# Attention ahead of two feed-forward layers on one core: scores in four two-bank units, transposes and products with v regrouped

## The chip, the cores and the metric

The kernel runs on one core of a Trainium2 chip. The metric is the device time of one execution in microseconds (us), the median of several runs. Engines are named as the profile names them: PE is the matrix engine (PEld its loading of weights), DVE the vector engine, ACT the scalar engine, POOL the GpSimd engine, SP the sync engine, which issues nearly all transfers here.

## What is computed

Attention with a decay per key (batch 4, 8 heads, 576 positions, 64 per head), then two feed-forward layers on the 2304 tokens, all in float32:

```python
scores = scale * q @ k.T                       # scale 1/8
cum = cumsum(log(clip(f, 1e-4, 1)))
scores = where(causal, -1e9, scores + cum[:, None] - cum[None, :])
attn = exp(scores - max(scores)); attn = attn / (sum(attn) + 1e-9)
x = attn @ v                                   # heads side by side: 2304 x 512
h = x @ w_in;  x = (h - tanh(h)) @ w_out       # 512 -> 2048 -> 512
h = x @ w_in2; out = (h * sigmoid(h)) @ w_out2
```

## The kernel before

Two heads make a pair, one on partitions 0 to 63 and one on 64 to 127; there are 16 pairs. The 576 queries of a head are cut into four tiles of 128 (i = 0 to 3; tile i sees 128(i+1) keys) and a last 64, and the last 64 of both heads share one tile, called i = 4, of 576 keys. So a pair has nine tiles, and the attention has 144. Each tile takes one step of a loop (`for n in range(N + LAG + 9)`, L643), and every engine works in the order in which this loop writes its instructions; nothing is reordered later.

A tile goes through these functions. `scores` (L429) and `scores_tail` (L440) multiply on PE in float32r: q and k are split in a high and a low part (`kqs`, made by `split` on POOL and DVE), and four products (high-high, high-low, low-high, decay rows) are added in PSUM. The two heads' products use 64 rows of the array each and run side by side. `least` (L452) adds the mask on DVE, copies the scores out of PSUM and finds the row's extreme. `expo` (L473) takes the exponential on ACT. `guard` and `normalise` (L480, L484) make the reciprocals of the row sums on DVE for three tiles at once, and POOL multiplies the tiles by them. `transposes` (L491) turns the tile in blocks of 128 x 128 on PE, nine steps after its scores (LAG = 9). `evac` (L514) copies them from PSUM to `ptf`, on ACT where i is 3 or 4, on DVE otherwise. `values` (L518) multiplies with v on PE with 64 columns of the array for each head, in four parts spread over nine steps, and `collect` (L530) copies the sums to x on ACT.

PSUM has eight banks: four of one tile each for scores (`ps_s`), two for transposes (`ps_t`), `misc` (half of tile 4's scores, and the first 64 queries' products with v) and `out_t`. A bank is written again when the instruction that reads it has ended. PE thus changes between three uses of its array: 64 rows for a head (scores), the whole array (transposes, tile 4, fillers, the layers) and 64 columns for a head (products with v).

Transfers are issued by SP in order: `load_kq` (608 KB a pair, `kqraw`), `load_v` (320 KB, `vraw`), `place_last` (the last 64 queries into `lq`, out of `kqs`), `place_dec` and `place_dec_last` (decay rows into `de` and `lq`). Pair 0 has its decay rows from `rows` in SBUF; these are also written to memory (`dec`), and all later pairs read them there. During the first nine steps `busy` puts idle matmuls of 512 columns between the steps of PE.

Weights come as float64 bits (512 KB for each half of a chunk, `raw`) and are decoded on ACT, DVE and POOL (`wstages`: L154 to L181) into high and low parts. Two chunks are decoded during the attention, three more from step 145 on, while the first hidden products (`hidden`, L256) already run between the last transposes; after the loop `front` and `project` (L315) follow without a break.

Of the kernel before, what the change touches and what calls it, by code (L numbers as in the profile page):

```python
# [23 lines left out]
LAG = 9  # L24
# [16 lines left out]
def forgetting_attention_two_ffn(  # L41
# [25 lines left out]
    def setup_masks(const):  # L67
# [9 lines left out]
        mask4 = const.tile([P, S // 2], F32, name="mask4")  # L77
        nc.gpsimd.memset(mask4, 0.0)
        for j in range(2):
            m = mask4[64 * j:64 * j + 64, S // 2 - 64:]  # L80
# [247 lines left out]
    def attention():  # L328
        with ExitStack() as actx:
# [8 lines left out]
            sp = pool(actx, "sp", LAG + 1)  # L338
# [7 lines left out]
            ps_s = pool(early, "ps_s", 4, space=PSUM)  # L346
# [11 lines left out]
            s4, out_0 = misc[:, 0:S // 2], misc[:, 448:512]  # L358
# [52 lines left out]
            def place_dec_last(p):  # L411
                for h in range(2):
                    to = rd(lqs[p % 2][64 * h:64 * h + 4, 2, half(h)])
                    c = slice(S + 512, 2 * S)
                    nc.sync.dma_start(out=to, in_=dec[2 * p + h, :, c] if p else rows[h:h + 1, :, c])

            order = [(0, 0), (1, 0), (0, 1), (1, 1), (2, 4), (0, 2), (1, 2), (0, 3), (1, 3)]
# [11 lines left out]
            def scores(p, i):  # L429

                n = P * (i + 1)
                q = slice(S + P * i, S + P * i + P)
                s = [ps_s.tile([P, 512], F32, tag="s", name=f"s{p}_{h}_{i}") for h in range(2)]
                for h in range(2):
                    sps[p, h, i] = (s[h][:, :n], mask[:, 512 - P * i:640])
                for r, (a, b) in enumerate(terms(*operands(p))):
                    for h in range(2):
                        nc.tensor.matmul(s[h][:, :n], a[half(h), q], b[half(h), 0:n], start=r == 0, stop=r == 3)  # L438

            def scores_tail(p, c0, c1):  # L440
                if c0 == 0:
                    dst = ps_s.tile([P, 512], F32, tag="s", name=f"s{p}_4")
                    dst = dst[:, 0:S // 2]
                    sps[p, 2, 4] = (dst, mask[:, 0:S // 2])
                else:
                    dst = s4
                hi, lo, de = operands(p)
                th, tl, td = (lqs[p % 2][:, j] for j in range(3))
# [264 lines left out]
```

## Time and profile before

| | us |
|---|---|
| median of 3 runs (lowest to highest) | 1006.44 (1005.3 to 1007.96) |
| the profiled execution, and its span | 1009.4, 1007.6 |
| PE busy | 993.6 |
| DVE busy | 574.6 |
| ACT busy | 452.8 |
| POOL busy, nearly all of it in the first 230 us | 182.5 |

The page of the profile gives busy time by engine and the chain of work that ended last; the timeline gives single instructions or runs of equal ones with their start and length, and in brackets the idle time of the engine just before them and who ended it. A matmul's length there includes the way through the array, so the time that a run of matmuls takes is read from its start to the start of the next run. The table of stretches gives busy time, count, granted clock of PE and the transfers for each stretch.

### The profile page before, as it was taken

Reading aid. Unit: us, or ns where it says so; the run is one execution under the profiler, and the core shown is the slowest. Engines: PE = TensorE matmul, PEld = TensorE weight load, DVE = VectorE, ACT = ScalarE, POOL = GpSimd, SP = SyncE. Lnnn points to the kernel's source line nnn. Section 1 sums busy time; section 2 is a strip of 40 time slices with the busy share of each in tenths; the row PEclk is TensorE's granted clock in tenths of the full one; section 3 lists DMA queues with packets and bytes.
Section 4 is the critical chain, followed back from the end, with each engine's and each line's share of the span. In section 5 each row is a group of like instructions: output and inputs, shape, how many; then the busy total and the mean of one; then the engine's idle time right before and its main releaser. Section 6 shows DMA issues by size and latency. Waiting matters only on the chain.

```text
span 1007.6 us, 13928 instructions
## 1 busy us (share of the span) xinstructions
PE 993.6 (99%) x5208; PEld 793.6 (79%) x5208; DVE 574.6 (57%) x1302; ACT 452.8 (45%) x963; POOL 182.5 (18%) x265
## 2 busy tenths in 40 slices
PE   8999999989999999999999999999999999999998
PEld 5666666658888888988889888888888888888887
DVE  6677778686667455755477773444353545623323
ACT  4666676745454433432344433434254333532222
POOL 6777888881000000000000000000000000000000
PEclk9899999999999999999999999999999999999999
DMA  5332222322112010111011120111110111001111
GB/s 163 132 120 85 86 88 86 113 87 82 52 75 84 1 43 26 59 42 43 1 67 60 49 78 1 42 42 43 43 42 1 42 42 43 1 1 42 42 43 63
DMA packets 21699, 56.67 MB, mean 56 GB/s; under 512 B 6848, under 2 KB 6848, under 8 KB 21600
## 3 DMA queue, kind: packets, MB, share of 16 engines
q1 hardware_dynamic: 21624, 55.77, 16.1%
q8 instruction: 41, 0.67, 0.3%
q14 instruction: 26, 0.21, 0.1%
q10 hardware_dynamic: 8, 0.02, 0.0%
HBM read 49.39 MB, written 5.31 MB: 54 GB/s over the span
## 4 chain that ended last, share of the span: by engine, by line
PE 95%; DMA 1%; POOL 1%; ACT 1%; DVE 1%; issue 1%; SPq 0%; POOLq 0%
PE a L315 39%; PE h L256 39%; PE t L498 6%; PE out_t L525 5%; PE s L438 5%; PE s L450 1%; PE misc L450 1%; DMA lq<-kqs 1%; DMA dec<-x 0%; PE misc L525 0%; POOL kqs L393 0%; ACT ptf L516 0%; DVE wb L168 0%; ACT p L475 0%; DVE wa L158 0%
## 5 line engine op out<-in xcount | busy, mean ns | idle before, releaser
L256 PE MATMUL h<-xh,wh 128*128 128x512 f32 (+1 forms) x640 | 236.8, 370 | 0.0
L256 PE MATMUL h<-xl,wh 128*128 128x512 f32 (+1 forms) x640 | 235.8, 368 | 0.0
L256 PE MATMUL h<-xh,wl 128*128 128x512 f32 (+1 forms) x640 | 235.7, 368 | 0.0
L278 DVE TENSOR_TENSOR gl<-g,gh 128x512 fp32r<-128x512 f32 (+1 forms) x158 | 101.4, 642 | 101.7 <-ACT gh L274 99.8
L256 PEld LDWEIGHTS h<-xh,wh 128*128 128x128 f32 x640 | 120.8, 189 | 24.7 <-issue 4.3
L256 PEld LDWEIGHTS h<-xl,wh 128*128 128x128 f32 x640 | 120.8, 189 | 20.1
L256 PEld LDWEIGHTS h<-xh,wl 128*128 128x128 f32 x640 | 120.7, 189 | 20.1
L274 ACT CAST gh<-g 128x512 fp32r<-128x512 f32 (+1 forms) x160 | 92.6, 579 | 94.8 <-DVE g L271 92.3
L315 PE MATMUL a<-gh,wh 128*128 128x512 f32 (+1 forms) x320 | 117.9, 369 | 0.0
L315 PE MATMUL a<-gl,wh 128*128 128x512 f32 (+1 forms) x320 | 117.8, 368 | 0.0
L315 PE MATMUL a<-gh,wl 128*128 128x512 f32 (+1 forms) x320 | 117.7, 368 | 0.0
L315 PE MATMUL a<-wh,gh 128*128 128x512 f32 x288 | 112.2, 390 | 0.0
L315 PE MATMUL a<-wl,gh 128*128 128x512 f32 x288 | 112.2, 390 | 0.0
L315 PE MATMUL a<-wh,gl 128*128 128x512 f32 x288 | 112.0, 389 | 0.0
L273 ACT ACTIVATE g<-h 128x512 f32<-128x512 f32 (+1 forms) x80 | 44.3, 553 | 113.6 <-PE h L256 98.5
L244 DVE TENSOR_TENSOR xl<-y,xh 128x512 fp32r<-128x512 f32 (+1 forms) x60 | 37.4, 638 | 96.6 <-ACT xh L242 96.6
L475 ACT ACTIVATE p<-p,mn 128x128 f32<-128x128 f32 (+3 forms) x128 | 71.9, 563 | 28.6 <-DVE mn L460 28.3
L242 ACT CAST xh<-y 128x512 fp32r<-128x512 f32 (+1 forms) x60 | 34.2, 580 | 104.8 <-PE h L256 103.1
L489 POOL TENSOR_SCALAR p<-p,sm 128x128 f32<-128x128 f32 (+3 forms) x128 | 69.0, 552 | 41.8 <-DVE sm L486 27.3
L244 DVE TENSOR_TENSOR xl<-x,xh 128x512 fp32r<-128x512 f32 (+1 forms) x56 | 34.5, 633 | 64.7 <-ACT xh L242 64.7
L516 DVE COPY ptf<-t 128x128 f32<-128x128 f32 (+2 forms) x112 | 43.7, 402 | 43.6 <-PE t L498 27.4
L315 PEld LDWEIGHTS a<-gh,wh 128*128 128x128 f32 x320 | 60.4, 189 | 10.2 <-ACT x L533 0.2
(100 smaller groups left out, 1458.6 us busy)
## 6 DMA issues: line engine op xcount, KB each, us to landing
raw<-w_in SPq DMA_DIRECT2D x32, 512.0 KB
raw<-w_out SPq DMA_DIRECT2D x32, 512.0 KB
kqraw<-kq SPq DMA_DIRECT2D x16, 608.0 KB
vraw<-v SPq DMA_DIRECT2D x16, 320.0 KB
out<-ob SPq DMA_DIRECT2D x18, 256.0 KB
lq<-kqs SPq DMA_DIRECT2D x32, 32.0 KB
dec<-x SPq DMA_DIRECT2D x1, 576.0 KB
de<-dec SPq DMA_DIRECT2D x30, 17.0 KB
```

What stands on the lines that cost most here:

```text
L244: eng.tensor_tensor(lo[:, :n], src[:, k, t0:t0 + n], rd(hi[:, :n]), ALU.subtract)
L256: nc.tensor.matmul(hp[:, :n], w[:, k * P:k * P + P], m[:, :n], start=(k == 0 and r == 0), stop=(k == NKT - 1 and r == 2),)
L273: nc.scalar.activation(g[:, :n], hp[:, :n], AF.Silu)
L274: nc.scalar.copy(gh[:, :n], g[:, :n])
L278: eng.tensor_tensor(gl[:, :n], g[:, :n], rd(gh[:, :n]), ALU.subtract)
L315: nc.tensor.matmul(dst, w, m, start=(first and r == 0), stop=(last and r == 2))
L438: nc.tensor.matmul(s[h][:, :n], a[half(h), q], b[half(h), 0:n], start=r == 0, stop=r == 3)
L475: nc.scalar.activation(pt[:, :w], pt[:, :w], AF.Exp, bias=mn, scale=-1.0, accum_out=sums[:, n // 3 % 5, n % 3, 0:1],)
L489: nc.gpsimd.tensor_scalar(pt[:, :w], pt[:, :w], sm[:, j:j + 1], 1.0, ALU.mult, ALU.mult)
L498: nc.tensor.transpose(tp[:, c, :], pt[:, c * P:c * P + P], ident)
L516: (nc.scalar.copy if t[2] >= 3 else nc.vector.tensor_copy)(dst, src)
L525: nc.tensor.matmul(dst, vraw[p][:, h, D * c:D * c + D], ptfs[p % 2][:, h, 448 * c + a:448 * c + q1], start=c == 0, stop=c == last,)
```

## The change

Scores are made in four units of two banks (`scores(p, u)`): unit 0 holds the four tiles of i = 0 and 1, unit 1 the two of i = 2, unit 2 the two of i = 3, unit 3 tile 4; there are two such buffers, and the tiles' order becomes units in turn, tile 4 last. The steps at which they are written are -1, 0, 4 and 6 of a pair. `least` handles tile 4 in one instruction of 576 columns, with a wider mask. The transposes of a unit are written together, into both banks of `ps_t`, at steps 13, 15, 17 and 18 after the pair's first tile, and copied out one step later by one DVE and one ACT instruction. Products with v come in two groups, at steps 22 (the first key block) and 26 (the others); for the last two pairs earlier. `load_v` of pair p stands at step 9p, the loads for pairs 1 and 2 stand earlier in the start, and pair 1 has its decay rows from `rows`, issued by SP before the write to `dec`. What SP is given at the start is written in another order, and the clearing of `lq` is done by POOL before it.

```diff
-            sp = pool(actx, "sp", LAG + 1)
+            sp = pool(actx, "sp", 2)
...
-            ps_s = pool(early, "ps_s", 4, space=PSUM)
+            ps_s = pool(early, "ps_s", 2, space=PSUM)
...
+            def decay(p, h, c):
+                r = 2 * p + h
+                return dec[r, :, c] if p > 1 else rows[r:r + 1, :, c]
...
-                        nc.sync.dma_start(out=to[64 * h:64 * h + 4], in_=dec[2 * p + h, :, c])
+                        nc.sync.dma_start(out=to[64 * h:64 * h + 4], in_=decay(p, h, c))
...
+                    nc.sync.dma_start(out=to, in_=decay(p, h, slice(S + 512, 2 * S)))
+
+            units = (((0, 0), (1, 0), (0, 1), (1, 1)), ((0, 2), (1, 2)), ((0, 3), (1, 3)), ((2, 4),))
+            order = [t for unit in units for t in unit]
...
+            def scores(p, u):
+
+                s = ps_s.tile([P, 2, 512], F32, tag="s", name=f"s{p}_{u}")
+                pt = pt4[p % 2] if u == 3 else sp.tile([P, (768, 768, 1024)[u]], F32, tag=f"p{u}", name=f"p{p}_{u}")
+                if u == 3:
+                    hi, lo, de = operands(p)
+                    th, tl, td = (lqs[p % 2][:, j] for j in range(3))
+                    for g in range(2):
+                        c = slice(S // 2 * g, S // 2 * g + S // 2)
+                        for r, (a, b) in enumerate(((th, hi), (th, lo), (tl, hi), (td, de))):
+                            nc.tensor.matmul(s[:, g, 0:S // 2], a, b[:, c], start=r == 0, stop=r == 3)
+                    sps[p, 2, 4] = (s[:, :, 0:S // 2], mask4.rearrange("p (g c) -> p g c", g=2), pt[:, 0:S])
+                    return
+                for i, c in ((0, 0), (1, P)) if u == 0 else ((u + 1, 0),):
+                    n = P * (i + 1)
+                    q = slice(S + P * i, S + P * i + P)
+                    for r, (a, b) in enumerate(terms(*operands(p))):
+                        for h in range(2):
+                            nc.tensor.matmul(
+                                s[:, h, c:c + n], a[half(h), q], b[half(h), 0:n], start=r == 0, stop=r == 3,
+                            )
+                c0 = 0
+                for h, i in units[u]:
+                    n, c = P * (i + 1), P if i == 1 else 0
+                    sps[p, h, i] = (s[:, h, c:c + n], mask[:, 512 - P * i:640], pt[:, c0:c0 + n])
+                    c0 += n
...
+            def transposes(p, u):
+
                 ptf = ptfs[p % 2]
-                for c in range(nch):
-                    nc.tensor.transpose(tp[:, c, :], pt[:, c * P:c * P + P], ident)
-                if i == 4:
+                tp = [ps_t.tile([P, 4, P], F32, tag="t", name=f"t{p}_{u}_{j}") for j in range(2)]
+
...
+                if u == 3:
+                    ptile.pop((p, 2, 4))
+                    pt = pt4[p % 2]
+                    for c in range(5):
+                        turn(c // 4, c % 4, pt, c)
...
+                pts = {t: ptile.pop((p,) + t)[0] for t in units[u]}
+                i = u + 1
+                for j in range(2 if u else 1):
+                    for h in range(2):
+                        for k in range(min(2, i + 1 - 2 * j)):
+                            turn(j, min(2, i + 1 - 2 * j) * h + k, pts[h, i], 2 * j + k)
...
+            def evac(p, u):
+                for j, (src, dst) in enumerate(tps.pop((p, u))):
+                    (nc.vector.tensor_copy if j == (u > 0) else nc.scalar.copy)(dst, src)
...
+            for t in lqs:
+                nc.gpsimd.memset(rd(t), 0.0)
...
             place_dec(0)
             for j in (2, 4, 3, 5):
                 split(0, j)
-            nc.vector.memset(rd(lqs[0]), 0.0)
+            place_dec(1)
+            load_kq(2)
+            place_last(0)
             place_dec_last(0)
-            place_last(0)
+            place_dec_last(1)
+            load_v(1)
             dec = dram.tile([BH, 4, 2 * S], F32, name="dec")
             nc.sync.dma_start(out=dec, in_=rows)
-            nc.gpsimd.memset(rd(lqs[1]), 0.0)
...
-                    later(n0 - 9, load_kq, p)
-                later(n0 - 1, place_dec, p)
-                later(n0 - 1, place_dec_last, p)
+                    if p > 2:
+                        later(n0 - 9, load_kq, p)
+                    later(n0 - 1, place_dec, p)
+                    later(n0 - 1, place_dec_last, p)
+                    later(n0 + (NTILE if p > 2 else 2 - NTILE), load_v, p)
...
-                later(n0 + (18 - NTILE if p > 2 else 0), load_v, p)
+
+            steps_ = (13, 15, 17, 18, 22, 23, 26, 27)
+            ends_ = {NP - 2: (13, 15, 17, 18, 20, 21, 21, 22), NP - 1: (11, 12, 13, 14, 16, 17, 17, 18)}
             for p in range(NP):
                 n0 = NTILE * p
-                for k, (h, i) in enumerate(order):
-                    if h == 0 and p + i:
-                        later(n0 + k - 2, scores, p, i)
-                    elif i == 4:
-                        later(n0 + k - 2, scores_tail, p, 0, S // 2)
-                        later(n0 + k - 1, scores_tail, p, S // 2, S)
-                m = n0 + NTILE + LAG + 1
-                at_ = (0, 3, 5, 7, 8) if p + 1 < NP else (0, 1, 2, 3, 4)
-                parts = ([(0, 0), (64, 0)], [(64, 1)], [(64, 2)], [(64, 3), (64, 4)])
-                for k, part in zip(at_, parts):
-                    later(m + k, values, p, part)
-                later(m + at_[0] + 1, collect, p, 0, 64)
-                later(m + at_[4], collect, p, 64, S)
+                for u, k in enumerate((-1, 0, 4, 6)):
+                    if p + u:
+                        later(n0 + k, scores, p, u)
+                k = ends_.get(p, steps_)
+                for u in range(4):
+                    later(n0 + k[u], transposes, p, u)
+                    later(n0 + k[u] + 1, evac, p, u)
+                later(n0 + k[4], values, p, [(0, 0), (64, 0)])
+                later(n0 + k[5], collect, p, 0, 64)
+                later(n0 + k[6], values, p, [(64, 1), (64, 2), (64, 3), (64, 4)])
+                later(n0 + k[7], collect, p, 64, S)
...
-            for n in range(N + LAG + 9):
-                if has(n - LAG):
-                    transposes(tiles[n - LAG])
-                run(n, scores, scores_tail, values)
-                if n < LAG - 1:
+            for n in range(N + 2 * NTILE):
+                if n % NTILE == 0:
+                    run(n, scores)
+                    run(n, transposes)
+                else:
+                    run(n, transposes)
+                    run(n, scores)
+                run(n, values)
+                if n < NTILE - 1:
                     busy(kqs[0][:, 0], 2)
-                if has(n - LAG - 1):
-                    evac(tiles[n - LAG - 1])
+                run(n, evac)
```

PE, in the middle of the attention, from a pair's first scores to those that follow (`s` scores by head and tile, after the change by unit; `t` transposes; `out_t` and `misc` products with v). Before:

```order
L438 MATMUL s_1_0_1006<-de_103 128x128
L498 MATMUL t_1_3_1021<-ident,p_1_3_854 128x128 x4
L525 MATMUL out_t<-ptf_110,vraw_364 64x192 x2
L525 MATMUL out_t<-ptf_110,vraw_364 64x64 x2
L498 MATMUL t_0_0_1045<-ident,p_0_0_880 128x128
L438 MATMUL s_0_1_1047<-kqs_885 128x256
...
L438 MATMUL s_1_1_1048<-de_103 128x256
L498 MATMUL t_1_0_1070<-ident,p_1_0_898 128x128
L525 MATMUL misc<-ptf_111,vraw_705 64x64 x2
L525 MATMUL out_t<-ptf_111,vraw_705 64x512 x2
L498 MATMUL t_0_1_1084<-ident,p_0_1_915 128x128 x2
```

and after the change:

```order
L450 MATMUL s_0_1105<-kqs_1001 128x256 x6
L450 MATMUL s_0_1105<-de_102 128x256 x2
L540 MATMUL out_t<-ptf_111,vraw_669 64x448 x2
L540 MATMUL out_t<-ptf_111,vraw_669 64x320 x2
L540 MATMUL out_t<-ptf_111,vraw_669 64x192 x2
L540 MATMUL out_t<-ptf_111,vraw_669 64x64 x2
L450 MATMUL s_1_1147<-kqs_1001 128x384 x6
L450 MATMUL s_1_1147<-de_102 128x384 x2
L493 MATMUL t_3_0_1157<-ident,pt_0_106 128x128 x4
L493 MATMUL t_3_1_1158<-ident,pt_0_106 128x128
L493 MATMUL t_0_0_1200<-ident,p_0_938 128x128 x4
L450 MATMUL s_2_1208<-kqs_1001 128x512 x6
```

Between two groups of scores there stood transposes, products with v and transposes again; now the products stand alone between units 0 and 1, and the transposes of tile 4 and of the next pair's unit 0 follow unit 1 together.

DVE in the same place (L460 and L463 are `least`, L516 and L531 `evac`, L387 and L386 a part of `split`). Before:

```order
L460 ISA p_0_0_1060,mn_0_0_1061<-s_0_0_1005,mask 128x128
...
L387 TENSOR_REDUCE kqs_1065<-kqraw_888 128x640
L516 COPY ptf_110<-t_0_0_1045 128x128
L460 ISA p_1_0_1078,mn_1_0_1079<-s_1_0_1006,mask 128x128
...
L516 COPY ptf_110<-t_1_0_1070 128x128
...
L460 ISA p_0_1_1097,mn_0_1_1098<-s_0_1_1047,mask 128x256
...
L516 COPY ptf_110<-t_0_1_1084 128x2x128
L460 ISA p_1_1_1124,mn_1_1_1125<-s_1_1_1048,mask 128x256
```

and after the change:

```order
L463 ISA p_0_1106,mn_0_0_1168<-s_0_1105,mask 128x128
...
L386 TENSOR_REDUCE kqs_1172<-kqraw_1004 128x640
L531 COPY ptf_110<-t_3_1_1158 128x2x64
L463 ISA p_0_1106,mn_1_0_1180<-s_0_1105,mask 128x128
...
L478 TENSOR_REDUCE sm_1184<-sums 128x3
L463 ISA p_0_1106,mn_0_1_1186<-s_0_1105,mask 128x256
...
L482 RECIPROCAL sm_1184<-sm_1184 128x3
L463 ISA p_0_1106,mn_1_1_1197<-s_0_1105,mask 128x256
...
L463 ISA p_1_1148,mn_0_2_1223<-s_1_1147,mask 128x384
```

Each copy of a transposed tile stood ahead of the next tile's `least`; now one copy, that of tile 4's last block, stands between the first and the second tile of unit 0, and the copy for unit 0 of the pair before follows behind the first tile of unit 1.

SP at the start, behind the first loads. Before:

```order
L409 DMA de_102<-x 2x1088 x2
L415 DMA lq_104<-x 4x1x64 x2
L398 DMA lq_104<-kqs_166 64x2x64 x2
L566 DMA dec<-x 32x4608
L405 DMA de_103<-dec 4x1088 x2
L415 DMA lq_105<-dec 4x64 x2
L373 DMA vraw_230<-v 128x640
L368 DMA kqraw_232<-kq 128x1216
L141 DMA raw_0_0_253<-w_in 128x1024
L398 DMA lq_105<-kqs_227 64x2x64 x2
```

and after the change:

```order
L412 DMA de_102<-x 2x1088 x2
L408 DMA de_103<-x 4x1x1088 x2
L367 DMA kqraw_187<-kq 128x1216
L397 DMA lq_104<-kqs_168 64x2x64 x2
L417 DMA lq_104<-x 4x1x64 x2
L417 DMA lq_105<-x 4x1x64 x2
L372 DMA vraw_195<-v 128x640
L586 DMA dec<-x 32x4608
L372 DMA vraw_253<-v 128x640
L140 DMA raw_0_0_255<-w_in 128x1024
L397 DMA lq_105<-kqs_238 64x2x64 x2
L140 DMA raw_0_1_306<-w_out 128x1024
```

The write to `dec` and what reads it moved behind the decay rows of pair 1, the third load of `kqraw` and the first copies to `lq`; that load, which stood ninth, is now the second.

## Rows read from the trace of the kernel before

**Rows 1.** Busy time by stretch: start, stretches 3 to 14, tail; columns are named.

```profile
core 0: us, PE busy (x) PEld busy (x) DVE busy (x) ACT busy (x) POOL busy (x), PEclk, DMA share, GB/s
9.43:46.54 37.11, 32.46 (x199) 22.35 (x198) 21.91 (x94) 17.63 (x55) 23.35 (x42) 0.86 0.47 151
46.54:186.06 139.52, 139.18 (x1066) 87.95 (x1065) 104.21 (x419) 95.72 (x285) 115.04 (x174) 1.00 0.27 87
199.35:223.79 24.44, 20.98 (x110) 11.86 (x110) 18.41 (x28) 13.35 (x28) 18.97 (x17) 0.93 0.25 87
```

**Rows 2.** Timeline of PE in one pair: start us, length us, engine, line, operation.

```profile
105.22 0.55 PE L438 MATMUL s<-kqs 64*128 64x128 f32 x6
...
105.82 0.66 PE L498 MATMUL t<-ident,p 128*128 128x128 f32 x4
...
107.25 0.62 PE L438 MATMUL s<-kqs 64*128 64x256 f32 x6
...
107.92 0.33 PE L498 MATMUL t<-ident,p 128*128 128x128 f32 x1
108.18 0.34 PE L525 MATMUL misc<-ptf,vraw 128*64 128x64 f32 x4
108.35 1.08 PE L525 MATMUL out_t<-ptf,vraw 128*64 128x512 f32 x4
109.36 0.44 PE L498 MATMUL t<-ident,p 128*128 128x128 f32 x2
...
111.00 0.79 PE L438 MATMUL s<-kqs 64*128 64x384 f32 x6
...
111.90 0.66 PE L498 MATMUL t<-ident,pt 128*128 128x128 f32 x4
112.48 0.97 PE L525 MATMUL out_t<-ptf,vraw 128*64 128x448 f32 x4
113.39 0.55 PE L498 MATMUL t<-ident,p 128*128 128x128 f32 x3
...
113.97 0.96 PE L438 MATMUL s<-kqs 64*128 64x512 f32 x6
...
115.10 0.55 PE L498 MATMUL t<-ident,p 128*128 128x128 f32 x3
```

**Rows 3.** Timeline of DVE in the same pair.

```profile
107.36 0.29 DVE L516 COPY ptf<-t 128x128 f32<-128x128 f32 x1 [0.18 <-PE t L498]
107.57 0.28 DVE L460 CUSTOM_DVE_ANT_0 p<-s,mask 128x128 f32<-128x128 f32 x1
...
108.56 0.41 DVE L460 CUSTOM_DVE_ANT_0 p<-s,mask 128x256 f32<-128x256 f32 x1
...
108.90 0.17 DVE L486 RECIPROCAL sm<-sm 128x3 f32<-128x3 f32 x1
```

**Rows 4.** Groups by line, pairs 3 to 14: count, busy us, mean ns, idle before.

```profile
L158 DVE TENSOR_SCALAR wa<-raw 128x512 uint32<-128x512 uint32 x4 | 1.9, 474 | 0.0
```

**Rows 5.** Timeline of DVE and PE around one wait of PE.

```profile
207.88 0.76 DVE L516 COPY ptf<-t 128x384 f32<-128x384 f32 x2 [0.56 <-PE t L511]
...
208.78 0.30 PE L498 MATMUL t<-ident,p 128*128 128x128 f32 x1 [0.24 <-DVE ptf L516]
```

**Rows 6.** Timeline of PE at the start.

```profile
14.84 0.63 PE L450 MATMUL s<-kqs,lq 128*128 128x288 f32 x3 [2.19 <-DMA lq<-kqs]
...
21.15 1.20 PE L551 MATMUL out_t<-kqs 128*128 128x512 f32 x4
...
27.25 1.06 PE L450 MATMUL s<-kqs,lq 128*128 128x288 f32 x3 [1.76 <-DMA lq<-kqs]
```

**Rows 7.** Timeline of SP at the start.

```profile
13.42 0.59 SPq L566 DMA_DIRECT2D dec<-x  x1
17.90 0.60 SPq L405 DMA_DIRECT2D de<-dec  x2
```

**Rows 8.** Timeline of POOL, its last row, in the tail.

```profile
226.31 3.00 POOL L181 TENSOR_TENSOR wl<-wl,wb 128x512 fp32r<-128x512 f32 x2
```

**Rows 9.** Timeline of PE: where the fifth hidden product starts.

```profile
232.17 0.39 PE L256 MATMUL h<-xh,wh 128*128 128x512 f32 x1
```

More of the change, by code (lines that the diff above doesn't have):

```diff
@@ L427, in terms @@
                 return (hi, hi), (hi, lo), (lo, hi), (de, de)
[L429 to L448, printed above, removed]
-                for r, (a, b) in enumerate(((th, hi), (th, lo), (tl, hi), (td, de))):
-                    nc.tensor.matmul(dst, a, b[:, c0:c1], start=r == 0, stop=r == 3)
+            def scores(p, u):
[23 more added lines that the diff above has]
+                    c0 += n
@@ L452, in least @@
             def least(t):
                 p, h, i = t
[L454 to L456 removed]
+                src, m, pt = sps.pop(t)
                 mn = small.tile([P, 1], F32, tag="mn", name=f"mn{p}_{h}_{i}")
[L459 to L463 removed]
@@ L514, in evac, with turn, place @@
-            def evac(t):
-                for src, dst in tps.pop(t):
-                    (nc.scalar.copy if t[2] >= 3 else nc.vector.tensor_copy)(dst, src)
+                    pt, _ = ptile[tiles[n + j]]
+                    nc.gpsimd.tensor_scalar(pt, pt, sm[:, j:j + 1], 1.0, ALU.mult, ALU.mult)
+            def transposes(p, u):
+                ptf = ptfs[p % 2]
+                tp = [ps_t.tile([P, 4, P], F32, tag="t", name=f"t{p}_{u}_{j}") for j in range(2)]
+                def turn(j, k, pt, c):
+                    nc.tensor.transpose(tp[j][:, k], pt[:, c * P:c * P + P], ident)
+                def place(j, c0, nc_, i):
+                    n = 2 * nc_
+                    q = P * i + 448 * c0
+                    dst = ptf[:, :, q:q + 448 * nc_] if nc_ > 1 else ptf[:, :, q:q + P]
+                    src = tp[j][:, 0:n]
+                    if nc_ > 1:
+                        dst = dst.rearrange("p h (c w) -> p h c w", w=448)[:, :, :, 0:P]
+                        src = src.rearrange("p (h c) w -> p h c w", h=2)
+                    return src, dst
+                if u == 3:
[3 more added lines that the diff above has]
+                        turn(c // 4, c % 4, pt, c)
+                    dst = ptf[:, :, 512:512 + 4 * 448].rearrange("p h (c w) -> p c h w", w=448)[:, :, :, 0:64]
+                    o = 448 * 4 + 512
+                    tps[p, u] = [
+                        (tp[0].rearrange("p c (h w) -> p c h w", h=2), dst),
+                        (tp[1][:, 0].rearrange("p (h w) -> p h w", h=2), ptf[:, :, o:o + 64]),
+                    ]
+                    return
+                pts = {t: ptile.pop((p,) + t)[0] for t in units[u]}
[4 more added lines that the diff above has]
+                            turn(j, min(2, i + 1 - 2 * j) * h + k, pts[h, i], 2 * j + k)
+                tps[p, u] = [place(j, 2 * j, min(2, i + 1 - 2 * j), i) for j in range(2 if u else 1)]
+                if u == 0:
+                    for h in range(2):
+                        turn(1, h, pts[h, 0], 0)
+                    tps[p, u].append(place(1, 0, 1, 0))
```

51 lines of the change are left out of this document (10 added, 41 removed).

## The prediction

> **What bounds the kernel now.** I read the table of stretches first. In the twelve pairs from the fourth to the fifteenth (46.54 to 186.06) PE is busy for 139.18 of 139.52 us at the full clock, 1.00 of 2.4 GHz, while DVE, ACT and POOL are busy for 104, 96 and 115 [rows 1]. So PE sets the time there, with 139.52 / 12 = 11.63 us a pair, and POOL is next with 115.04 / 12 = 9.6. The layers behind 223.79 are not touched by the change and keep PE busy; only when they can start matters. At the start, 9.43 to 46.54, PE idles for 4.65 of 37.11 us and its mean clock is 0.86 [rows 1]; two of these waits, 2.19 and 1.76 us, are for the copies to `lq` [rows 6]. In the tail, between the 145th step (199.35) and the first product of `project`, PE idles for 3.5 of 24.44 us while DVE and POOL are busy for 18.4 and 19.0 [rows 1].
>
> Second, the timeline of PE, read from start to start. One transpose alone takes 0.26 us (107.92 to 108.18), four take 0.58 (111.90 to 112.48) [rows 2]: another one costs 0.11, and 0.15 goes with the change of the array's use on either side. The 448-column product with v takes 0.91 (112.48 to 113.39) and the 512-column one 1.01 (108.35 to 109.36) [rows 2], so 0.0016 per column, and again some 0.2 of a block does not grow with its size. Before, a pair has 16 such changes between scores, whole-array work and products with v; after, seven. This is why a PE that looks full can still give time back.
>
> **The steady pairs, PE alone.** Same products, fewer blocks [rows 2]. Unit 0: 0.60 (105.22 to 105.82) + 0.67 (107.25 to 107.92), less one joint of 0.2, 1.07. Products with v on key blocks 1 to 4: 1024 columns against 448, 0.91 + 576 x 0.0016 = 1.83. Unit 1: 0.90 (111.00 to 111.90). Transposes of tile 4 and of the next unit 0: 0.26 + 10 x 0.11 = 1.36. Unit 2: 1.13 (113.97 to 115.10). `misc` and the first key block: 1.18 (108.18 to 109.36). The rest was four transposes and the eight products of tile 4, 1.64 (109.36 to 111.00), and has ten transposes more: 2.74. Sum 10.2 against 11.63. A direct change from scores to products with v does not occur before; I take the same price as for the others (bounds 0 and 0.4).
>
> **The steady pairs, with the waits that the change adds.** There are two buffers of two banks, so unit 2 may be written only when `least` has read the four tiles of unit 0; and on DVE the copy of tile 4's last transposed block stands between the first and the second of these tiles. DVE works in order, so the copy, which waits for PE, holds three `least`, which PE then waits for. From the start of unit 0 on PE: unit 0, the products with v and unit 1 take 1.07 + 1.83 + 0.90 = 3.80; five transposes end at about 3.80 + 0.77 = 4.57 (length of four, 0.66, and 0.11 [rows 2]). Then DVE, by starts: copy 0.21 (107.36 to 107.57), tile of 128 columns 0.20 (its 0.28 less the overlap of 0.08 that the others show), tile of 256 0.34 (108.56 to 108.90), the last one in full, 0.41 [rows 3], and 0.15 for the short reduce and reciprocal: 1.31. From the end of a copy on DVE (207.88 + 0.76) to PE's start (208.78) are 0.14 [rows 5]; 0.04 for the way to DVE is an estimate, below that. Unit 2 starts at 4.57 + 0.04 + 1.31 + 0.14 = 6.06, while PE is through with the transposes before it at 5.8 (they wait for the same copy). Then 1.13 + 1.18 + 2.74 = 5.05 up to the next unit 0: **11.1 us a pair**, not 10.2. I checked what else could be late there: unit 0 of the next pair needs the tiles of unit 2 read by then (about 10.4, one 256-column copy and a tile of 512 after the transposes of unit 1); unit 1 needs tile 4 read (11.2, wanted at 14.9); POOL's split for it ends some 1.8 us ahead. So 12 pairs x (11.63 - 11.1) = 6.4 us saved. Of the decoding of two chunks, two DVE instructions (one of L158, 474 ns in the mean [rows 4], and one of its kind, L168, taken at the same) fall between copy and tiles; a full PE hid them, now they cost 1.0. The sixteenth pair, 186.06 to 199.35 before, 13.3, takes 11.1: 2.2 saved. Bounds for the period: 10.9 and 11.5, as the signals and the joint come out.
>
> **What stays hidden.** DVE has three copies less (four instead of seven) and one instruction for tile 4 instead of two, ACT has one copy more; ACT is busy for 96 of 139.52 [rows 1], and what it copies is wanted by PE only after the next wait for DVE. POOL clears `lq` before the masks and so begins later with its part of pair 0's split, which only unit 1 needs, about 1 us after unit 0. `load_v` at step 9p waits for products of pair p - 3 that stand right before it and holds the next `kqraw` load on SP; that load is wanted a pair later.
>
> **The start.** Pair 0 begins at 9.43 in both; pair 3 begins at 46.54 before. After: unit 0 with its wait for the decay rows 2.0 (as before, estimate), units 1 to 3 0.9 + 1.13 + 1.1, fillers in groups of 8, 4 and 4 by the 1.14 that four take (21.15, next block 22.29) 4.4: pair 1 at 18.9. The copies to `lq` for unit 3 are issued 11 to 13, behind one load of 608 KB, and wanted at 16.5; before, scores of tile 4 came ahead of i = 2 and 3 and stood waiting [rows 6]. Pair 1: 1.07 + 0.9 + 0.8 + 0.5 (the wait of unit 2) + 1.13 + 0.8 + 1.1 + 1.0 = 7.3, pair 2 at 26.2. It reads its decay rows from `dec`; from the issue of that write to SP's next instruction, which waits for its landing, are 17.90 - 13.42 = 4.5 us [rows 7]. It is now issued at about 16, behind pair 1's rows, so the rows are asked for at 21 and there by 25. Pair 2 has no products of key blocks 1 to 4 to do: 11.1 - 1.83 = 9.3, pair 3 at 35.7. Saved: 10.8, of which 3.95 are the two waits, the rest the low clock that followed them, fillers and changes. Bounds: 4 (only those waits) and 13.
>
> **The tail.** PE gets there sooner and has less to wait for: the products of the last pair stand at steps 7 and 8 behind the last tile, and no longer behind a `collect` that waits on ACT. But the fifth chunk is decoded on POOL until 226.31 + 3.00 = 229.3 [rows 8], 30.0 after step 145, and the fifth hidden product starts at 232.17 [rows 9], 32.8 after it. POOL and DVE have the same work there, so I let PE come no earlier than that: 2.8 saved. Bounds: 0, and 6 if the decoding, too, was held by PE's waits.
>
> **The sum**, against the profiled execution (1009.4, of which 1.8 lie around the span, and 3.0 over the median): 10.8 + 6.4 - 1.0 + 2.2 + 2.8 = 21.2, so 988.2; from the median, 1006.4 - 21.2 = 985.2, say **985**.
>
> **Rivals.** *PE alone sets the pace*: the copy finds DVE ready and the order costs nothing, 10.2 a pair. Thirteen pairs x 0.9 less than 985.2: 974. For it: DVE has a quarter of its time free; against: the order itself. *Another engine takes over* and the period stays at 11.63: POOL needs 9.6 [rows 1] and a group of three tiles waits for a reciprocal that DVE makes late; 6.4 + 0.5 lost, 992. If the start, too, gives only its two waits, 999; with no gain in the tail either 1002, near the edge of no change. *Slower, by the clock*: the change adds two waits of PE to every pair, 0.7 and 0.25 us. Where PE waited at the start, the granted clock was 0.86 over the stretch, against 1.00 in the pairs without waits [rows 1]. If the steady pairs went to a mean of 0.80, the part of the period that is PE's (11.1 less the 1.49 of DVE and its signals, 9.6) becomes 12.0 and the period 13.5: 12 x 1.87 + 0.2 more, plus 1.0, less 10.8 at the start, with no gain in the tail: 1019. It decides from a period of 12.7, a mean clock of 0.86. Against it: in the tail PE idled for 14% of the stretch and still had 0.93 [rows 1]. The Trainium skill has this as a rule (TensorE: Matmul & The Clock Gate, "A second HAM failure mode: psum-queue depth-cycling"): a kernel whose matrix engine idles briefly between groups as it goes round PSUM's banks can swing between both clock levels and lose throughput. The stretches of before bear it out only for waits of about 2 us.
>
> **How the numbers follow.** Forecast 0.60; PE alone 0.12; another engine 0.16; no change 0.06; the clock 0.06. Within 0.3% is about what a measurement of this kernel can tell from no change. Faster 0.88, same 0.06, slower 0.06. The range takes in PE alone and the bounds of the terms (start 4, period 11.5, tail 0: 1001): 974 to 1001.
>
> **What would show it.** In the new trace pairs 4 to 15 should start 11.1 apart, PE should wait before unit 2 for a DVE `least` by about 0.2 and before the transposes of unit 0 for the copy by about 0.7, and pair 3 should start near 36. A period near 10.2 means that the chain through DVE was misread; one near 11.6 with PE waiting for POOL, the second rival; a granted clock under 1.00 between 40 and 170, the third. It goes wrong most easily at the start, where the terms hang on transfers that pass each other on SP's queue.

## The result, and the profile after

| us | before | after |
|---|---|---|
| median of 4 runs (lowest to highest) | 1007.2 (1005.3 to 1009.34) | 990.54 (988.36 to 991.65) |
| profiled execution, and its span | 1009.4, 1007.6 | 991.6, 989.8 |

The ratio of after to before is 0.9831, with a 95% interval of 0.9802 to 0.986: faster by 16.7 us. The forecast was 985 with a range of 974 to 1001. In the profiled executions, to which the sum was made, 21.2 us were forecast and 17.8 came. Of the four runs after, the two near 991.6 had a mean granted clock of 0.998, the two at 988.36 and 989.46 one of 1.000; the profiled execution is one of the first two.

The stretches of [rows 1] have these counterparts: the start up to pair 3's first scores, the twelve pairs behind it, and the tail from the first hidden product to the first product of `project` (columns as in [rows 1]).

```profile
core 0: us, PE busy (x) PEld busy (x) DVE busy (x) ACT busy (x) POOL busy (x), PEclk, DMA share, GB/s
9.80:38.81 29.01, 25.14 (x190) 19.45 (x190) 18.62 (x77) 18.30 (x59) 23.18 (x41) 0.94 0.60 192
38.81:172.20 133.39, 125.98 (x1069) 88.90 (x1068) 92.96 (x361) 99.08 (x298) 114.30 (x174) 1.00 0.28 92
185.76:204.43 18.67, 18.14 (x113) 11.95 (x111) 11.62 (x22) 11.98 (x24) 12.12 (x12) 1.00 0.28 96
```

PE is no longer full in the steady pairs: 125.98 of 133.39 us, at a clock of 1.00. Where the idle time lies, the timeline of PE in one pair shows (for [rows 2]), from unit 0 at 49.86 to the next at 60.90:

```profile
49.86 0.55 PE L450 MATMUL s<-kqs 64*128 64x128 f32 x6
...
50.98 1.95 PE L540 MATMUL out_t<-ptf,vraw 128*64 128x448 f32 x16
52.86 0.79 PE L450 MATMUL s<-kqs 64*128 64x384 f32 x6
...
53.76 0.77 PE L493 MATMUL t<-ident,pt 128*128 128x128 f32 x5
55.00 0.85 PE L493 MATMUL t<-ident,p 128*128 128x128 f32 x6 [0.47 <-DVE ptf L531]
55.93 0.95 PE L450 MATMUL s<-kqs 64*128 64x512 f32 x6
...
60.90 0.55 PE L450 MATMUL s<-kqs 64*128 64x128 f32 x6
```

From one unit 0 to the next are 11.04. Five transposes of tile 4 start at 53.76 and those of unit 0 at 55.00, behind a wait of 0.47 for a copy on DVE. DVE in the same place, for [rows 3]:

```profile
54.56 0.29 DVE L531 COPY ptf<-t 128x128 f32<-128x128 f32 x1 [2.33 <-PE t L493]
54.77 0.28 DVE L463 CUSTOM_DVE_ANT_0 p<-s,mask 128x128 f32<-128x128 f32 x1
...
55.05 0.41 DVE L463 CUSTOM_DVE_ANT_0 p<-s,mask 128x256 f32<-128x256 f32 x1
...
55.48 0.40 DVE L463 CUSTOM_DVE_ANT_0 p<-s,mask 128x256 f32<-128x256 f32 x1
```

DVE has nothing to do for 2.33 us, since its next instruction is the copy of tile 4's last block and PE hasn't made it. The three tiles of unit 0 that stand behind it are in PSUM since about 51, when PE went on to the products with v. This is the chain of the forecast, row by row. All of PE's waits in the twelve pairs:

```profile
engine line waited for: us in total, times, longest us
PE t L493 <- DVE ptf L531: 5.2, 11, 0.5
PE s L450 <- DVE mn L463: 0.8, 2, 0.4
PE t L493 <- POOL kqs L384: 0.5, 1, 0.5
```

Twelve times 0.47 before the transposes of unit 0 (one of them put down to POOL) and twice, in pairs with decoding, a visible wait before unit 2.

### The profile page after: what moved, and what is told of

Read it like the earlier page. It is cut to its first block, busy times and chain, and to the rows that moved or that the text cites. A ratio compares the mean times of both kernels' runs of the same rounds, so it can differ in the third digit from the quotient of the medians.

```text
span 989.8 us, 13833 instructions
## 1 busy us (share of the span) xinstructions
PE 970.7 (98%) x5208; PEld 792.1 (80%) x5208; DVE 556.7 (56%) x1221; ACT 456.8 (46%) x979; POOL 183.7 (19%) x266
## 4 chain that ended last, share of the span: by engine, by line
PE 94%; DVE 3%; POOL 1%; DMA 1%; issue 1%; ACT 0%; SPq 0%; POOLq 0%; DVEq 0%; ACTq 0%
PE a L314 39%; PE h L255 39%; PE s L450 5%; PE out_t L540 4%; PE t L493 4%; PE s L442 2%; DVE p L463 1%; PE out_t L568 1%; DMA lq<-kqs 1%; POOL wl L176 0%; DVE ptf L531 0%; PE misc L540 0%; POOL wl L180 0%; DMA raw<-w_in 0%; DVE wa L157 0%
## 5 line engine op out<-in xcount | busy, mean ns | idle before, releaser
L314 PEld LDWEIGHTS a<-gl,wh 128*128 128x128 f32 x320 | 60.3, 189 | 10.1
```

The costliest lines, as they stand in the source:

```text
L314: nc.tensor.matmul(dst, w, m, start=(first and r == 0), stop=(last and r == 2))
```

## Experiments

Each kernel is the changed one with one edit, unless said otherwise. All times are medians; 990.54 stands for the changed kernel, whose runs spread over 3.3 us. The kernel before, run again with each group of experiments, had medians of 1006.42 to 1007.93, so a difference of some 1.5 us between two medians says nothing; there the profiles have to decide.

### The two waits of the steady pair

**Products with v over the copy.** Key blocks 1 to 4 go between the transposes of tile 4 and those of unit 0.

```diff
-            steps_ = (13, 15, 17, 18, 22, 23, 26, 27)
+            steps_ = (13, 15, 17, 18, 22, 23, 27, 28)
```

> Edit against the changed kernel: the products with v on key blocks 1 to 4 one step later (27 instead of 26), so that PE has them between the transposes of tile 4 and those of unit 0, and scores of units 0 and 1 stand together. Seven changes of the array's use a pair as before the edit. Theory (PE waits only because the copy of tile 4's last block, and the tiles behind it on DVE, come back late): in the changed kernel 42.70 to 43.95 is 1.25 us for five transposes that need 0.53, and 43.95 to 44.88 is 0.93 for six that need 0.64, 1.0 us of waiting in a pair; 1.88 us of products now lie over the copy, both waits go, the period falls from 11.05 to about 10.05, and the decoding's 0.8 us is hidden again: 12 x 1.0 + 0.8 + about 1 in pairs 1, 2 and 16, so about 977 us against 990.5. Rival (another engine would hold PE at 11.05 anyhow): the period stays at 10.8 or more, PE waits elsewhere for POOL or ACT, 988 to 991.

Measured: 978.95 us, ratio to before 0.973 (0.9704 to 0.9755). PE in one pair, and the stretch of the twelve pairs:

```profile
88.56 0.77 PE L493 MATMUL t<-ident,pt 128*128 128x128 f32 x5
89.25 1.95 PE L540 MATMUL out_t<-ptf,vraw 128*64 128x448 f32 x16
91.14 0.88 PE L493 MATMUL t<-ident,p 128*128 128x128 f32 x6
91.94 0.50 PE L450 MATMUL s<-kqs 64*128 64x512 f32 x2
```

```profile
35.73:158.32 122.59, 122.59 (x1071) 88.26 (x1070) 94.76 (x361) 97.84 (x298) 114.36 (x174) 1.00 0.30 100
```

PE is busy for 122.59 of 122.59 us; no wait is left. From one unit 0 to the next most pairs take 10.19. That is the 10.2 which the prediction worked out for PE alone, and 0.86 less than 11.05, not the 1.0 of the expectation. There, the 0.93 from the start of unit 0's six transposes to unit 2 was set against 0.64 for six transposes ahead of tile 4, where the array's use doesn't change. With that change of use, and without a wait, the same six take 0.80 (91.14 to 91.94), so unit 2 waited 0.13, not 0.29. The time missed the expected 977 by 2 us with it. The rival (another engine holds PE at 11.05) is out: POOL with 114.36 us of work in 122.59 still keeps up.

**The copy behind three tiles.** Only the copies of tile 4 move, by two steps.

```diff
-                    later(n0 + k[u] + 1, evac, p, u)
+                    later(n0 + k[u] + (3 if u == 3 and p < NP - 2 else 1), evac, p, u)
```

> Edit against the changed kernel: the two copies of tile 4's transposes stand two steps later on DVE and ACT, so DVE has three tiles of unit 0 ahead of the copy and only the last behind it. Theory (two separate waits): the wait of the transposes of unit 0 for the copy, 0.72, is the way there and back and stays; the wait of unit 2 for the tiles behind the copy, 0.29, goes. Period 10.75 to 10.8, about 986.5 us. Rival (unit 2 waits for something else, or the copy comes later because DVE isn't through with three tiles): period 11.05 or more, 990 us or more.

Measured: 987.64 us, pairs of 10.9. PE, and then DVE, in one pair:

```profile
84.24 0.77 PE L493 MATMUL t<-ident,pt 128*128 128x128 f32 x5
85.48 0.85 PE L493 MATMUL t<-ident,p 128*128 128x128 f32 x6 [0.47 <-POOL p L485]
86.26 0.96 PE L450 MATMUL s<-kqs 64*128 64x512 f32 x6
```

```profile
85.05 0.29 DVE L531 COPY ptf<-t 128x128 f32<-128x128 f32 x1 [1.11 <-PE t L493]
85.25 0.41 DVE L463 CUSTOM_DVE_ANT_0 p<-s,mask 128x256 f32<-128x256 f32 x1
```

The first wait is the same: 1.24 us from tile 4's transposes to those of unit 0, 0.47 of them idle. Here the profile puts it down to POOL, but of the twelve such waits from pair 3 on (36.69 to 167.63) it puts ten down to DVE's copy, at the same length, and here too the copy ends just ahead of PE, at 85.34. The second wait is gone: 0.78 from unit 0's transposes to unit 2, against 0.93. So the two waits are separate as the theory said, and the second was worth 0.15, half of what was expected. With the 0.71 of the first (1.24 less the 0.53 that five transposes need; 185.24 to 185.76 in the changed kernel, where PE doesn't wait) this makes up the whole 0.86.

**What a block costs.** Products with v in three groups instead of two.

```diff
-                later(n0 + k[6], values, p, [(64, 1), (64, 2), (64, 3), (64, 4)])
+                if p < NP - 2:
+                    later(n0 + 24, values, p, [(64, 1), (64, 2)])
+                    later(n0 + k[6], values, p, [(64, 3), (64, 4)])
+                else:
+                    later(n0 + k[6], values, p, [(64, 1), (64, 2), (64, 3), (64, 4)])
```

> Edit against the changed kernel: the products with v on key blocks 1 to 4 in two groups, blocks 1 and 2 at step 24 (between tile 4's scores and the transposes of unit 2), blocks 3 and 4 at step 26. Two more changes of the array's use in a pair and the same products. Theory (a block's own price is about 0.2 us whatever its size): period 11.2 to 11.3 instead of 11.05, about 993 us. Rival (changes cost nothing by themselves, only waits do): period 11.05 or lower, since a shorter group ahead of unit 1 lets the transposes start sooner; 990 us.

Measured: 993.36 us, most pairs of 11.34 to 11.37. PE, from one unit 0 to the next:

```profile
86.09 0.55 PE L450 MATMUL s<-kqs 64*128 64x128 f32 x6
...
97.43 0.55 PE L450 MATMUL s<-kqs 64*128 64x128 f32 x6
```

The wait for the copy is as before (1.23 from 88.69 to 89.92). The same products in one block more, with two changes more of the array's use, cost 0.31 a pair, 0.15 a change between the whole array and 64 columns; the rival (changes are free) is out. The Trainium skill says of this (TensorEngine Tiling (Array Packing), "Key Properties") that a change of the tiling mode, not of the tile, drains TensorE. It gives no price; this run does for its kind of change.

### The start

**Two loads later.**

```diff
-            for n, k, m in ((2, 0, 0), (6, 0, 1), (12, 1, 0), (16, 1, 1), (135, 2, 0), (136, 2, 1),
+            for n, k, m in ((5, 0, 0), (6, 0, 1), (12, 1, 0), (16, 1, 1), (135, 2, 0), (136, 2, 1),
...
-                    later(n0 + (NTILE if p > 2 else 2 - NTILE), load_v, p)
+                    later(n0 + (NTILE if p > 2 else 6 - NTILE), load_v, p)
```

What it is about: in the changed kernel PE waits 2.42 us in pair 1 and then runs at half clock (0.50 from 28 to 30; eight transposes take 1.84 instead of 1.03). PE there, which [rows 6] show of before, and SP ahead of it, as in [rows 7]:

```profile
26.12 0.63 PE L442 MATMUL s<-kqs,lq 128*128 128x288 f32 x3 [2.42 <-DMA lq<-kqs]
...
27.25 1.84 PE L493 MATMUL t<-ident,p 128*128 128x128 f32 x8
```

```profile
15.86 0.44 SPq L372 DMA_DIRECT2D vraw<-v  x1
16.36 0.42 SPq L586 DMA_DIRECT2D dec<-x  x1
16.82 0.42 SPq L372 DMA_DIRECT2D vraw<-v  x1
17.29 2.19 SPq L140 DMA_DIRECT2D raw<-w_in  x1
19.59 2.08 SPq L397 DMA_DIRECT2D lq<-kqs  x2
```

The copies to `lq` (19.59) stand behind 320, 576, 320 and 512 KB.

> Edit against the changed kernel: SP issues the first 512 KB of weights and the 320 KB of v for pair 2 behind the copies to lq for pair 1 instead of ahead of them. Theory (these copies, asked for at 19.59 and there at 26.12, stand behind 0.8 MB that the transfer engines, 0.8 to 1.1 busy from 18 to 26, carry first): PE's wait of 2.42 us before tile 4 of pair 1 goes or falls under 0.5, the stretch at half clock behind it (26 to 31) too, pair 3 starts at 34.8 to 35.5 instead of 38.81, and the time is about 986.8. Rival (the copies are late for their own long way from the split, or SP's issue): the wait stays above 1.5 us and the time within 1 us of 990.5.

Measured: 989.45 us, not to be told from 990.54, and not the 986.8 of the theory. PE, and the granted clock in the column ahead of the last two:

```profile
23.48 0.64 PE L442 MATMUL s<-kqs,lq 128*128 128x288 f32 x3
...
25.62 0.55 PE L450 MATMUL s<-kqs 64*128 64x128 f32 x6
27.50 0.57 PE L450 MATMUL s<-de 64*128 64x128 f32 x2 [1.33 <-DMA de<-dec]
```

```profile
26.00:30.00 4.00, 2.67 (x26) 2.22 (x25) 1.36 (x4) 1.14 (x3) 3.59 (x8) 0.91 0.95 322
30.00:34.00 4.00, 3.52 (x17) 2.42 (x15) 3.20 (x17) 3.21 (x12) 2.82 (x5) 0.50 0.72 254
```

The wait for `lq` went, as the theory said, and pair 2 started at 25.62 instead of 29.02. But then PE waited 1.33 us for pair 2's decay rows, now behind the loads that had moved, and the clock was at half (0.50) from 30 to 34; pair 3 started at 39.12. The theory named one transfer; with that one early, the next was late.

**All four weight loads later.**

```diff
-            for n, k, m in ((2, 0, 0), (6, 0, 1), (12, 1, 0), (16, 1, 1), (135, 2, 0), (136, 2, 1),
+            for n, k, m in ((20, 0, 0), (24, 0, 1), (30, 1, 0), (34, 1, 1), (135, 2, 0), (136, 2, 1),
```

> Edit against the changed kernel: the four weight loads of 512 KB that stood at steps 2, 6, 12 and 16 stand at steps 20, 24, 30 and 34; they are decoded from step 40 on. Theory (in the first 35 us whatever PE needs next stands behind bulk transfers: the copies to lq in the changed kernel, the decay rows of pair 2 when only two loads were moved, the next kqraw in the run with three groups): with 2 MB out of the way none of these waits is over 0.5 us, the clock stays at 1.00 after 20, pair 3 starts at 35 to 36.2 instead of 38.81, and the time is about 987.5. Rival (the way from the write to dec to its reading, or the splits, set the start): a wait of over 1 us for the decay rows or for POOL, pair 3 at 38 or later, 990.

Measured: 987.87 us, and the four runs lie between 987.56 and 987.98. All waits of PE between 16 and 40:

```profile
16.59 0.63 PE L442 MATMUL s<-kqs,lq 128*128 128x288 f32 x3 [0.17 <-DMA lq<-kqs]
...
22.08 0.96 PE L450 MATMUL s<-kqs 64*128 64x512 f32 x6 [0.64 <-DVE mn L463]
...
29.07 0.84 PE L493 MATMUL t<-ident,p 128*128 128x128 f32 x6 [0.47 <-DVE ptf L531]
```

```profile
17.80 2.80 SPq L397 DMA_DIRECT2D lq<-kqs  x2
```

The copies to `lq` are issued at 17.80 and PE doesn't wait for them; the 0.64 at 22.08, for DVE, the changed kernel has as well. Pair 3 starts at 34.98, the clock stays at 1.00, and the runs of this kernel spread over 0.4 us instead of 3.3; so they do in the two kernels below that have this edit as well (0.3 and 0.4). By the times alone the gain isn't clear: the ratio to before is 0.9813 (0.9797 to 0.983), that of the changed kernel 0.9831 (0.9802 to 0.986). By the profile and the spread, the weight loads in the way were the cause, and they also made the changed kernel's runs differ. Whether by their bytes or by SP's time to issue them is open for `lq`, whose copies now go out 1.8 us earlier (17.80, not 19.59). For pair 2's decay rows it was what stood ahead of them: with two loads moved they were asked for at 21.69 and there at 27.50; here they are asked for at 22.13, and PE doesn't wait for them at 26.39. The Trainium skill (DMA: Bandwidth & Descriptors, "Queues, rings and completion order") says that SP's transfers share one ring on each DMA engine, whose descriptors are taken in order. The changed kernel's trace fits that: 64 KB, issued from 19.59 on behind these loads, let PE go on at 26.12.

**The start as before**, with the units as changed.

```diff
-                return dec[r, :, c] if p > 1 else rows[r:r + 1, :, c]
+                return dec[r, :, c] if p > 0 else rows[r:r + 1, :, c]
...
-            for t in lqs:
-                nc.gpsimd.memset(rd(t), 0.0)
...
-            place_dec(1)
-            load_kq(2)
-            place_last(0)
+            nc.vector.memset(rd(lqs[0]), 0.0)
             place_dec_last(0)
-            place_dec_last(1)
-            load_v(1)
+            place_last(0)
...
-                    if p > 2:
-                        later(n0 - 9, load_kq, p)
-                    later(n0 - 1, place_dec, p)
-                    later(n0 - 1, place_dec_last, p)
-                    later(n0 + (NTILE if p > 2 else 2 - NTILE), load_v, p)
+                    later(n0 - 9, load_kq, p)
+                later(n0 - 1, place_dec, p)
+                later(n0 - 1, place_dec_last, p)
+                later(n0 + (NTILE if p > 2 else 0), load_v, p)
```

> Edit against the changed kernel: the start as before the change (pair 1's decay rows read from dec, load_kq(2) and the loads of v at their old steps, lq cleared on DVE for pair 0 and on POOL after the write to dec for pair 1); units, transposes and products as changed. Theory (the start's gain is mostly the new order of what SP is given): dec is read at 17.9 at the earliest and pair 1's unit 0 wants its rows at 18.8, so PE waits 2.5 to 4 us there, and again for lq in pair 1; pair 3 starts at 42 to 44 instead of 38.81, about 994.5. Rival (the gain is from units that ask for lq later and from fewer fillers): pair 3 at 39 to 40, 990 to 991.5.

Measured: 994.27 us, pair 3 at 41.13. PE, and DVE between:

```profile
19.82 0.61 PE L450 MATMUL s<-de 64*128 64x128 f32 x2 [0.83 <-DMA de<-dec]
...
25.83 1.65 PE L450 MATMUL s<-kqs 64*128 64x512 f32 x6 [3.37 <-DVE mn L463]
```

```profile
23.94 0.82 DVE L386 TENSOR_REDUCE kqs<-kqraw 128x640 fp32r<-128x640 f32 x1 [2.65 <-DMA kqraw<-kq]
24.67 0.28 DVE L463 CUSTOM_DVE_ANT_0 p<-s,mask 128x128 f32<-128x128 f32 x1
```

The time fits the theory, its places don't: the decay rows cost 0.83 us instead of 2.5 to 4, PE doesn't wait for `lq` in pair 1, and pair 3 comes ahead of the 42 to 44. The long wait, 3.37, is before unit 2, whose buffer DVE can't empty because its part of the split, standing ahead of three `least`, waits 2.65 us for the third `kqraw`. So of the 7.7 us that the changed kernel gains up to pair 3, the start's new order (loads, decay rows and clearing together) has about 2.3 (41.13 to 38.81) in the profiles and 3.7 in the medians. The rest, 46.54 to 41.13, is put down to the units and fewer fillers by subtraction; no run takes these apart.

### The tail

**The last two pairs at the steps of the others.**

```diff
-            ends_ = {NP - 2: (13, 15, 17, 18, 20, 21, 21, 22), NP - 1: (11, 12, 13, 14, 16, 17, 17, 18)}
+            ends_ = {}
...
-            for n in range(N + 2 * NTILE):
+            for n in range(N + 2 * NTILE + 1):
```

> Edit against the changed kernel: the last two pairs keep the steps of all others for transposes and products with v (the loop runs a step longer). Theory (the tail's gain is from these steps: products of the last pair not behind the last step): the last products stand at steps 157 and 161 behind all hidden products, PE waits for copies that stand behind decoding on DVE and ACT, as before the change, and the first product of project starts 3 to 6 us later than 204.43; the waits for POOL's weights after it vanish, so that 2 to 4 us stay: 992.5 to 994.5. Rival (the gain is from grouping alone): 990 to 991.5.

Measured: 992.2 us, just under the range of the theory; with runs from 988.86 to 994.35 it can't be told from 990.54, so only the profile tells what the steps do. PE in the tail:

```profile
200.72 1.33 PE L493 MATMUL t<-ident,pt 128*128 128x128 f32 x5 [2.71 <-DVE ptf L531]
...
207.82 0.50 PE L314 MATMUL a<-gh,wh 128*128 128x512 f32 x1
```

A wait of 2.71 us, half clock behind it (0.52 from 202 to 204) as in the tail before (0.50 from 219 to 221), and 36.3 us from pair 15 (171.57) to the first product of `project`, against 32.2 with the earlier steps (172.20 to 204.43). From the first hidden product on there are 22.7 us (185.12 to 207.82) against 18.67, and 24.44 before: in these executions the steps give 4.0 of the 5.8 us, grouping alone 1.7. Of the 4.0, 1.6 come back behind it, where in the changed kernel PE waits for decoded weights. Those rows of the changed kernel, PE and POOL:

```profile
208.48 0.50 PE L255 MATMUL h<-xh,wl 128*128 128x512 f32 x1 [0.71 <-POOL wl L180]
...
214.74 0.50 PE L255 MATMUL h<-xh,wl 128*128 128x512 f32 x1 [0.52 <-POOL wl L180]
```

```profile
203.03 1.30 POOL L277 TENSOR_TENSOR gl<-g,gh 128x512 fp32r<-128x512 f32 x1 [3.49 <-ACT gh L273]
...
206.97 2.90 POOL L180 TENSOR_TENSOR wl<-wl,wb 128x512 fp32r<-128x512 f32 x2
...
212.96 2.98 POOL L180 TENSOR_TENSOR wl<-wl,wb 128x512 fp32r<-128x512 f32 x2
```

**The gate behind the decoding.** POOL idles 3.49 us up to 203.03 for the second gate's input, with decoding queued behind.

```diff
-            at(8, gate, 1)
+            at(11, gate, 1)
```

> Edit against the changed kernel: the gate of the second hidden group of the first layer is written at step 11 of the tail instead of 8, behind more of the decoding of weights. Theory (the two waits of PE for POOL's wl, which begin at 207.6 and 214.1 and cost 1.5 us with what the next matmul loses, come from decoding that is queued on POOL behind this gate, for whose input POOL idles 3.49 us up to 203.03): the waits go or fall under 0.3 and the time falls by 1.2 to 1.6, to about 989.1. Rival (decoding is held by DVE or by the weights' transfers): waits as before the edit, or a new one for gl, 990.5 or more.

Measured: 989.96 us, not to be told from 990.54. Of the two waits one stays, and it is longer:

```profile
215.22 0.50 PE L255 MATMUL h<-xh,wl 128*128 128x512 f32 x1 [1.22 <-POOL wl L180]
```

From the first product of `project` to PE's last, 781.34 us instead of 781.65. The theory took one queue for the chain: POOL, no longer held by the gate, now waits 1.03 us for DVE's part of the decoding (to 204.20) and 1.62 for the gate (to 208.85). What would bring the last decoded weights forward stays open.

### Both edits that worked

```diff
-            for n, k, m in ((2, 0, 0), (6, 0, 1), (12, 1, 0), (16, 1, 1), (135, 2, 0), (136, 2, 1),
+            for n, k, m in ((20, 0, 0), (24, 0, 1), (30, 1, 0), (34, 1, 1), (135, 2, 0), (136, 2, 1),
...
-            steps_ = (13, 15, 17, 18, 22, 23, 26, 27)
+            steps_ = (13, 15, 17, 18, 22, 23, 27, 28)
```

> Both edits that moved their own wait, together: products with v on key blocks 1 to 4 at step 27, and the four weight loads at steps 20, 24, 30 and 34. Theory (the two are independent, one acts in every pair, the other ahead of pair 3): period 10.2, pair 3 at 34 to 35, no wait over 0.7 us after 20, granted clock 1.00; 978.95 less 0.7 to 1.7 that the first edit's run still lost ahead of pair 3 (35.73): 977.3 to 978.3, with a spread of under 1 us. Rival (weights that come with the second and third pair collide there): a wait of over 1 us between 30 and 70, 979 or more.

Measured: 977.75 us (977.56 to 977.83), ratio to before 0.9715 (0.9702 to 0.9728). Pair 3 starts at 34.59, and from 40 to 157 PE is never idle:

```profile
40.00:157.00 117.00, 117.00 (x1016) 84.25 (x1015) 90.65 (x343) 94.43 (x288) 109.92 (x166) 1.00 0.34 112
```

With the gate moved as well:

> The two edits and, in the tail, the second gate of the first layer at step 11 instead of 8. Alone this last edit took away one of PE's two waits for POOL's wl and lengthened the other from 0.52 to 1.22, and the stretch from project's first product to the end fell from 781.65 to 781.34. Theory: 0.3 us less than the two edits together, which can't be told from none. Rival (the earlier tail makes room for the decoding): 1 us or more less.

Measured: 977.74 us, no difference, as expected.

## Why the prediction was right, and where it was off

| saved, in the profiled executions | forecast | measured |
|---|---|---|
| up to pair 3 | 10.8 | 46.54 - 38.81 = 7.7 |
| pairs 4 to 15, with decoding | 6.4 - 1.0 = 5.4 | 139.52 - 133.39 = 6.1 |
| sixteenth pair, up to the first hidden product | 2.2 | 13.29 - 13.56 = -0.3 |
| tail, up to `project` | 2.8 with what follows | 24.44 - 18.67 = 5.8 |
| behind it, to the end of the span | | 783.8 - 785.4 = -1.6 |
| sum | 21.2 | 17.7 |

By the spans the sum is 17.8: the steady pairs and the tail gave 2.1 more than forecast, the start and the sixteenth pair 5.6 less. Of the 5.3 us between 985.2 and 990.54, 3.4 are this shortfall; the other 1.9 are no step: the profiled execution of before lay 3.0 above its median at the time, that of after 1.1 above its own. Two readings of the prediction are off by little. It cut before's stretch of twelve pairs at 186.06, but the sixteenth pair's scores start there at 186.61; cut alike in both kernels, the twelve pairs gave 140.07 - 133.39 = 6.7 and the sixteenth 12.74 - 13.56 = -0.8, with the same sum. And the bounds of its terms add up to 1000, not 1001.

**The steady pairs were right**, in size and in mechanism. PE alone was worked out at 10.2 and measures 10.19 (with the copy covered); with DVE's chain 11.1, and it is 11.05. The wait before unit 0's transposes was put at 0.7 and is 0.71; the one before unit 2 at 0.25 and is 0.13 to 0.15. The decoding costs 133.39 - 12 x 11.05 = 0.8 instead of 1.0. The step that decided was to follow DVE's order past one copy; an argument from busy time alone (DVE idle for a quarter of the time) gives the rival's 974, and the runs with the products moved show what that order costs: 133.39 - 122.59 = 10.8 us in the twelve pairs, and 987.87 - 977.75 = 10.1 between the two kernels with late weights.

**The start was 3.1 short.** The failed step is "The copies to `lq` for unit 3 are issued 11 to 13, behind one load of 608 KB", which was applied to pair 0 alone, where it held. For pair 1 the prediction weighed the decay rows, and took the copies to `lq` for no issue. They came at 26.12, behind 1.7 MB. Without the weights in the way pairs 1, 2 and 3 start at 18.74, 26.00 and 34.98, where 18.9, 26.2 and 35.7 were forecast: the terms were right, and the transfers between them were missing. What they cost differs from run to run. With the same start, the wait for these copies was 2.42 us in the changed kernel's profile, 1.49 in that of the copy behind three tiles (pair 3 at 36.69) and 0.94 in that of the products moved (35.73), the last two without a fall of the clock. So the 3.1 belongs to one execution, and where 35.7 was met with the weights in the way it was luck.

**The sixteenth pair was mis-sized.** "takes 11.1: 2.2 saved" compared a pair up to the next unit 0 with a stretch up to step 145. Behind the last pair there is no unit 0, but the products with v of the fourteenth pair stand in that place (183.36, 1.95 long), and transposes of tile 4 behind them. 11.1 and these are the 13.56.

**The tail gave 4.2 instead of 2.8**, net of the wait for decoded weights. That POOL's decoding sets the floor was right (PE does wait for it now, 0.71 and 0.52), and so was its end: 212.96 + 2.98 = 215.94, 30.2 behind the first hidden product, where 30.0 was taken. Wrong was "so I let PE come no earlier than that": the fifth hidden product starts at 213.60, ahead of that end, with products that need no `wl`, and then waits only for the first of POOL's last two instructions (up to 214.74). Undoing the early steps costs 4.0 up to `project`.

**The rivals.** Another engine (11.63) is excluded by v's products moved, where POOL keeps up with 10.19. The slower one, by the clock, did not come: with a wait of 0.47 in each pair the granted clock stays at 1.00 over 133 us. So the rule of the Trainium skill that the prediction names (TensorE: Matmul & The Clock Gate, "A second HAM failure mode: psum-queue depth-cycling"), on short idle times that recur, did not show at this size. The clock fell only behind single longer waits in the start and, with the old steps, in the tail.

## What to carry to other kernels

An engine with time to spare can still set the pace by its order: look for an instruction that waits for the bounding engine and holds others for which that engine waits, and put independent work of the bounding engine over that way there and back (here 10 to 11 us for one number). Where a start is full of transfers, moving the load that is waited for can just pass the wait to the next one, as here; take out what isn't needed yet, which also steadied the runs. Where blocks of different use of the array alternate, count the changes; here two of them cost 0.31 us.

## What the runs showed of the hardware

A wait of 1.33 us, 0.64 us of waiting some 5 us before it, was followed by half clock from 30 to 34 in one run; 1.49 us, with 0.64 before it and 0.81 five us later, left the clock at 1.00 in another (the kernel with the copy behind three tiles). So the length of a wait alone didn't decide it here. Of the waits for `lq` in pair 1, with the same start, 0.94 and 1.49 left the clock at 1.00, and the 2.42 of the changed kernel was followed by 0.50 from 28 to 30.
